# A 7-product block scheme for h = y w_in, with h kept in DRAM, in a fused attention and two-MLP kernel

## The chip, the cores and the metric

The kernel runs on one core of one Trainium2 chip. The metric is the device time of one execution in microseconds (us). PE is TensorE (matmul), DVE VectorE, ACT ScalarE, POOL GpSimd, and SP the engine that issues most DMAs. Each engine, and each DMA queue, works through its own instructions in order.

## What is computed

```
x = attention(q, k, v)      # 4 batches, 8 heads, 576 positions, head size 64, window of 64 -> 2304 tokens x 512
a = x @ w1; b = x @ w2      # 512 x 1024 each
y = ((a * b) @ w3) @ w_out  # 1024 x 1024, 1024 x 512
h = y @ w_in                # 512 x 2048
g = maximum(0.01 * h, h)
out = g @ w_out2            # 2048 x 512 -> 2304 x 512
```

The inputs q, k, v are float32, the weights are 64-bit floats, the output is float32.

## The kernel before

Outside the attention every matrix product is formed from split operands: a float32 value is stored as a rounded high part (fp32r) and the remainder as a low part, and `mm3` issues three matmuls, high x low, high x high, low x high, into one PSUM tile. A split is one copy on ACT (high) and one subtraction on DVE (low). The 64-bit weights are converted on the chip in units of 128 x 512 values: a DMA (`raw`, 512 KB), one ACT scaling (`f`), two bit operations and one shift on DVE, then the split. `advance` moves this pipeline by one unit.

The program has four parts in order:

1. A front of some 150 us: attention of batch 0, w3 w_out folded into one matrix (`wf`), w1 and w2 converted.
2. Four batches of 16 steps. A step is half a batch (288 tokens) and one of eight 128-row tiles f: `ab_step` for a, `ab_step` for b, and with a lag of two steps `y_step`, which adds this tile's share into four PSUM tiles of y. Three `slot()` calls in a step issue the pieces of the next batch's attention; for batches 1 to 3 the transposed probabilities go through DRAM (`pd` out, `pts` in, on SP), and the matmul `pa` that uses them is issued five slots after the store. After the eighth tile ACT copies the four y tiles into `io` tiles (two buffers) and ACT's queue stores them to `yd` in DRAM.
3. In the last batch, which has no attention beside it, w_in and w_out2 are converted (32 units), and the loads and splits of the first y block begin.
4. For six blocks of 384 tokens and 16 tiles f of the 2048 columns: `h_step` (12 matmuls of 384 columns, then ACT scaling, DVE maximum, ACT copy, DVE subtraction, which gives g) and two steps later `o_step` (9 matmuls of 512 columns). Blocks 0 and 1 are interleaved. At the end of a block ACT or DVE copies the output tiles into `io`; the last block's three tiles go into buffers of another pool (`xtile`).

The order of the instructions on an engine follows the order of the calls, moved by priorities (`first`, `high_priority`) and a scheduler.

Of the kernel before, what the change touches and what calls it, by code (L numbers as in the profile page):

```python
# [20 lines left out]
def tile_kernel(ctx: ExitStack, tc: tile.TileContext, q, k, v, w1, w2, w3, w_out, w_in, w_out2, out):  # L21
# [12 lines left out]

    nc = tc.nc
    B, H, S, D = q.shape
    T = B * S
# [17 lines left out]
    W2N = 4  # L55
# [20 lines left out]
    wpool = ctx.enter_context(tc.tile_pool(name="wpool", bufs=1))  # L76
    dram = ctx.enter_context(tc.tile_pool(name="dram", bufs=1, space=bass.MemoryType.DRAM))

    yd = dram.tile([P, KD, T], F32, name="yd")

    stage = tc.alloc_tile_pool(name="stage", bufs=2, side="right")
    att = tc.alloc_tile_pool(name="att", bufs=2, side="right", reuse_waits="tile")
# [3 lines left out]
    xpool = tc.alloc_tile_pool(name="xpool", bufs=8)  # L86
# [21 lines left out]
    def xtile():  # L108
        return xpool.tile([P, 2, S], F32R, name="x", tag="x")
# [8 lines left out]
    def raw_tiles(n):  # L118

        if 0 < n < NHP - 1:  # L120
            t = xpool.tile([P, 2, S], F32, name="x", tag="x")
            return t[:, 0], t[:, 1]
        return tuple(att.tile([P, S], F32, name=x, bufs=1) for x in ("qin", "kin"))
# [8 lines left out]
    def loads_v(n):  # L132
        b, hp = divmod(n, NHP)
        if n < NHP and n >= 2:
            vt = xpool.tile([P, 2, 2, (S - W) // P, D], F32, name="x", tag="x")
        else:
            vt = att.tile([P, 2, 2, (S - W) // P, D], F32, name="vt", bufs=2)
# [62 lines left out]
    def tp(g):  # L200
# [5 lines left out]
        sp.dma_start(pd, tb)  # L206
# [5 lines left out]
    def av(g):  # L212
# [11 lines left out]
        if (b, hp) not in xt:  # L224
            xt[b, hp] = xtile()
# [6 lines left out]
    def wslot(key):  # L232
        pl, tag, bufs = wpool, "w", 8
        if key[0] in ("win", "wo2") and key[1] < W2N // 2:
            pl, tag, bufs = pb1, "w2", W2N
        elif key[0] == "wf" or key[0] in ("win", "wo2") and key[1] >= KF2 // 2 - 2:
# [24 lines left out]
    def feed():  # L261

        while n_of["load"] < min(len(units), n_of["bits"] + RAW):
            load_unit()

    def load_unit():
# [3 lines left out]
        return sp.dma_start(u["raw"], u["src"]).ins  # L270
# [4 lines left out]
    def advance(stop):  # L275

        now = dict(n_of)
        if now["scale"] < min(stop, now["load"]):
# [4 lines left out]
            act.mul(u["f"], u["hi"].bitcast(F32), 2.0 ** -112)  # L283
# [78 lines left out]
    for p in range(KF2 // 2):  # L362
        col_units(w_in, "win", p)
        for h in range(2):
            row_unit(w_out2, "wo2", 2 * p + h)
# [91 lines left out]
    def ab_step(b, hf, f, j):  # L457
# [8 lines left out]
        if j == 0:  # L466
            pss["a"] = gp.tile([P, NH], F32, name="a32", tag="a32", bufs=1)
            with first():
                act.copy(pss["a"], ps)
# [26 lines left out]
    ysp = {}  # L496

    def load_y(c, kk):
        ysp[c, kk] = pb1.tile([P, NB2], F32, name="yr", bufs=1)
        sp.dma_start(ysp[c, kk], yd[:, kk, c * NB2:(c + 1) * NB2])  # L500

    def split_y(c, kk):
        yr, t = ysp[c, kk], xtile()
        act.copy(t[:, 0, 0:NB2], yr)
        dve.tensor_tensor(out=t[:, 1, 0:NB2], in0=yr, in1=f32(t[:, 0, 0:NB2]), op=ALU.subtract)
        ysp[c, kk] = t

    ysteps = []
    for b in range(B):
        if b + 1 < B:  # L510
            plan_att(b + 1, *((10, 26) if b == 0 else (1, 37)))
        for s in range(2 * KF):
# [6 lines left out]
            if b == B - 1:  # L519
                for _ in range(2):  # L520
                    advance(len(units))
                if 4 <= s < 4 + KD:
                    load_y(0, s - 4)
                if 5 <= s < 5 + KD:
                    split_y(0, s - 5)
# [8 lines left out]
        if b == B - 2:  # L534
            att.release()
            ps_at.release()
            ps_h = tc.alloc_tile_pool(name="ps_h", bufs=2, space=PSUM, side="right", reuse_waits="tile")
            pb1 = tc.alloc_tile_pool(name="pb1", bufs=W2N, side="right", reuse_waits="tile")
# [3 lines left out]
    gp.release()  # L542
    ps_mm.release()
    ps_ab.release()
    pb2 = tc.alloc_tile_pool(name="pb2", bufs=2, reuse_waits="tile")
    ps2 = tc.alloc_tile_pool(name="ps2", bufs=6, space=PSUM, reuse_waits="tile")


    g_t = {}

    def h_step(c, f):
        ps = ps_h.tile([P, NB2], F32, name="h")
        w = cols2(slots["win", f // 2])
        ws = slice(P * (f % 2), P * (f % 2) + P)
        with tc.issue_after(pss["last"]) if c == 0 and f < 2 else nullcontext():
            for kk in range(KD):
                y = ysp[c, kk]
                mm3(ps, w[:, 0, kk, ws], w[:, 1, kk, ws], y[:, 0, 0:NB2], y[:, 1, 0:NB2], kk == 0, kk == KD - 1)
# [82 lines left out]
```

## Time and profile before

| quantity | value |
|---|---|
| median of 3 runs | 888.66 us (888.52 to 888.69) |
| profiled execution | 888.87 us |
| its span (first to last instruction) | 887.1 us |
| PE busy | 847.2 us, 96% |
| DVE busy | 466.9 us, 53% |
| ACT busy | 338.7 us, 38% |
| POOL busy | 43.5 us, 5% |
| mean granted TensorE clock | 0.987 of full speed |

The span leaves out 1.8 us of the profiled execution. Matmuls overlap, so that their durations add up to more than the time they take together: the spacing from start to start (the pitch) is what one costs in a full stream. The same holds, more weakly, for DVE.

### The profile page before, as it was taken

Reading aid. Unit: us, or ns where it says so; the run is one execution under the profiler, and the core shown is the slowest. Engines: PE = TensorE matmul, PEld = TensorE weight load, DVE = VectorE, ACT = ScalarE, POOL = GpSimd, SP = SyncE. Lnnn points to the kernel's source line nnn. Section 1 sums busy time; section 2 is a strip of 40 time slices with the busy share of each in tenths; the row PEclk is TensorE's granted clock in tenths of the full one; section 3 lists DMA queues with packets and bytes.
Section 4 is the critical chain, followed back from the end, with each engine's and each line's share of the span. In section 5 each row is a group of like instructions: output and inputs, shape, how many; then the busy total and the mean of one; then the engine's idle time right before and its main releaser. Section 6 shows DMA issues by size and latency. Waiting matters only on the chain.

```text
span 887.1 us, 14660 instructions
## 1 busy us (share of the span) xinstructions
PE 847.2 (96%) x5476; PEld 778.1 (88%) x5476; DVE 466.9 (53%) x1231; ACT 338.7 (38%) x890; POOL 43.5 (5%) x61
## 2 busy tenths in 40 slices
PE   5779787999999999999999999999999999999997
PEld 3568686999999999999999899999899999999996
DVE  7999898763665365539298922233223223223222
ACT  4466653442434243436165622233223223222221
POOL 1012000110111011100000000000000000000000
PEclk9899998899999999999999999999999999999999
DMA  7897668666555444415256300012001001000000
GB/s 239 214 208 225 168 183 196 173 163 134 125 113 137 98 105 103 113 46 182 71 168 203 100 0 1 1 30 88 27 1 44 28 1 36 28 1 13 24 0 36
DMA packets 166822, 84.84 MB, mean 96 GB/s; under 512 B 133216, under 2 KB 153184, under 8 KB 166752
## 3 DMA queue, kind: packets, MB, share of 16 engines
q1 hardware_dynamic: 162144, 79.20, 33.8%
q10 hardware_dynamic: 4608, 4.72, 1.6%
q8 instruction: 43, 0.70, 0.3%
q14 instruction: 27, 0.22, 0.1%
HBM read 67.37 MB, written 16.52 MB: 95 GB/s over the span
## 4 chain that ended last, share of the span: by engine, by line
PE 81%; DMA 8%; DVE 5%; SPq 2%; ACT 2%; issue 1%; DVEq 0%; ACTq 0%
PE o L72 7%; PE o L73 7%; PE o L71 7%; PE h L73 7%; PE h L71 7%; PE h L72 7%; PE ab L71 7%; PE ab L73 6%; PE ab L72 6%; PE mm L71 4%; PE mm L73 4%; PE mm L72 4%; PE sc L168 3%; DMA raw<-in_moe_w_dram 3%; PE pa L222 2%; DMA raw<-in_moe_w_out_dram 2%
## 5 line engine op out<-in xcount | busy, mean ns | idle before, releaser
L71 PE MATMUL ab<-x,w 128*128 128x288 f32 x512 | 154.7, 303 | 5.1 <-ACT x L228 3.0
L563 DVE TENSOR_TENSOR t<-h,t 128x384 f32<-128x384 f32 x95 | 52.9, 557 | 197.2 <-ACT t L562 197.2
L72 PE MATMUL ab<-x,w 128*128 128x288 f32 x512 | 152.3, 297 | 0.0
L73 PE MATMUL ab<-x,w 128*128 128x288 f32 x512 | 152.2, 297 | 0.0
L562 ACT ACTIVATE t<-h 128x384 f32<-128x384 f32 x95 | 46.7, 491 | 192.9 <-PE h L73 191.3
L71 PEld LDWEIGHTS ab<-x,w 128*128 128x128 f32 x512 | 97.4, 190 | 7.0 <-ACT x L228 3.1
L72 PEld LDWEIGHTS ab<-x,w 128*128 128x128 f32 x512 | 97.3, 190 | 0.2
L73 PEld LDWEIGHTS ab<-x,w 128*128 128x128 f32 x512 | 97.3, 190 | 0.1
L73 PE MATMUL h<-x,w 128*128 128x384 f32 x288 | 97.0, 337 | 0.0
L71 PE MATMUL h<-x,w 128*128 128x384 f32 x288 | 96.9, 336 | 0.0
L72 PE MATMUL h<-x,w 128*128 128x384 f32 x288 | 96.8, 336 | 0.0
L71 PE MATMUL o<-w,g 128*128 128x512 f32 x213 | 83.3, 391 | 1.0 <-ACT g L564 1.0
L72 PE MATMUL o<-w,g 128*128 128x512 f32 x213 | 84.2, 395 | 0.0
L73 PE MATMUL o<-w,g 128*128 128x512 f32 x213 | 82.6, 395 | 0.0
L565 DVE TENSOR_TENSOR g<-t,g 128x384 fp32r<-128x384 f32 x95 | 53.0, 558 | 45.8 <-ACT g L564 45.8
L71 PE MATMUL mm<-ab,wf 128*128 128x288 f32 x256 | 70.7, 310 | 3.9 <-ACT ab L475 3.9
L283 ACT ACTIVATE f<-raw 128x512 f32<-128x512 f32 x72 | 48.5, 677 | 67.7 <-DMA raw<-in_moe_w_dram 33.1
L73 PE MATMUL mm<-ab,wf 128*128 128x288 f32 x256 | 74.2, 296 | 0.0
L72 PE MATMUL mm<-ab,wf 128*128 128x288 f32 x256 | 74.2, 295 | 0.0
L564 ACT CAST g<-t 128x384 fp32r<-128x384 f32 x95 | 48.7, 513 | 51.6 <-DVE t L563 51.5
L176 ACT ACTIVATE s<-s,nm 128x128 f32<-128x128 f32 x144 | 56.5, 395 | 19.9 <-DVE nm L172 18.7
L474 DVE TENSOR_TENSOR p<-ab,a 128x288 f32<-128x288 f32 x64 | 29.1, 454 | 55.7 <-PE ab L73 53.4
(93 smaller groups left out, 1586.3 us busy)
## 6 DMA issues: line engine op xcount, KB each, us to landing
raw<-in_moe_w_dram SPq DMA_DIRECT2D x32, 512.0 KB, 4.6
raw<-in_moe_w_out_dram SPq DMA_DIRECT2D x24, 512.0 KB, 4.8
raw<-in_moe_w_in_dram SPq DMA_DIRECT2D x16, 512.0 KB, 3.9
vt<-in_v_dram SPq DMA_DIRECT2D x56, 128.0 KB, 2.9
pd<-tb SPq DMA_DIRECT2D x36, 192.0 KB, 2.2
pts<-pd SPq DMA_DIRECT2D x144, 48.0 KB, 2.0
yd<-io ACTq DMA_DIRECT2D x32, 144.0 KB, 2.5
yr<-yd SPq DMA_DIRECT2D x24, 192.0 KB, 2.4
```

The lines of the kernel that those rows point to most:

```text
L71: pe.matmul(ps, lhsT=lh, rhs=rh, start=first, stop=False)
L72: pe.matmul(ps, lhsT=lh, rhs=rl, start=False, stop=False)
L73: return pe.matmul(ps, lhsT=ll, rhs=rh, start=False, stop=last).ins
L168: pe.matmul(sc[:, t, :], lhsT=qb[:, t, :], rhs=kT[n][:, k0:k0 + P], start=True, stop=True)
L176: act.activation(out=s[:, t, :], in_=s[:, t, :], func=AF.Exp, bias=nm[:, t:t + 1], scale=-1.0, accum_out=sm[:, t:t + 1])
L222: pe.matmul(o[W * h:W * h + W, W * t:W * t + W], lhsT=vt[:, a, h, m, :], rhs=pts[:, 2 * h:2 * h + 2, t], start=True, stop=True)
L283: act.mul(u["f"], u["hi"].bitcast(F32), 2.0 ** -112)
L474: dve.tensor_tensor(out=p32, in0=ps, in1=pss["a"], op=ALU.mult)
L562: act.mul(t, ps, 0.01)
L563: dve.tensor_tensor(out=t, in0=ps, in1=t, op=ALU.max)
L564: act.copy(g[:, 0], t)
L565: dve.tensor_tensor(out=g[:, 1], in0=t, in1=f32(g[:, 0]), op=ALU.subtract)
```

## The change

The matrices of h = y w_in are cut into blocks. A quad is a pair of adjacent 128-column tiles of w_in (8 pairs `p`) by a pair of 384-token blocks (3 pairs `c`), and the contraction of 512 is cut into two halves. Of such a 2 x 2 by 2 x 2 block product the standard form has 8 block products; the change uses the 7-product form with 4 sums of w_in blocks, 4 sums of y blocks and 7 sums after the products. A product is 6 matmuls of 384 columns.

- `keep`: 28 units (all 16 of w_in, 12 of the 16 of w_out2) are converted but not split. They are stored as float32 in DRAM (`wd`), from step 4 of the third batch on. The other 4 are converted while output is formed.
- `w_ops(p)`: loads two units, forms 4 sums in `io` tiles, splits 7 blocks. `y_ops(c, j)`: loads four y blocks, forms 4 sums, splits 7 blocks, with the low parts on POOL for the last token pair. For the first token pair and the first w_in pair they stand in the steps of the last batch.
- `Quad.step`: one product, and the additions into float32 tiles `c`, out of PSUM, on DVE (the first one a copy on ACT); finished blocks of h are stored to `hd` by SP.
- After all 24 quads come the 96 output steps: `ahead` loads h four steps ahead, splits g two steps ahead, and loads and splits the kept w_out2 rows in the steps of block 0. `o_step` is as before, but the last block's tiles go through `io` as well.
- Buffers: the x tiles are in two pools of four (`xa`, `xb`), and other pools are released earlier.

```diff
+    def keep(i):
+        return lambda f: sp.dma_start(wd[i], f)
...
-            if b == B - 1:
-                for _ in range(2):
-                    advance(len(units))
...
+            if 2 * KF * b + s >= 2 * KF * (B - 2) + 4:
+                for _ in range(2 if b == B - 1 and s < 4 else 1):
+                    advance(KEPT)
+            if b == B - 1 and n_of["fin"] == KEPT and len(early) > 0:
+                early.pop(0)()
...
+    def y_ops(c, j):
...
+        for o, x0, x1 in ((t1, b12, b11), (t2, b22, t1), (t3, b22, b12), (t4, b21, t2)):
+            dve.tensor_tensor(out=o, in0=x0, in1=x1, op=ALU.subtract)
+        for i, x in enumerate((b11, b21, b22, t1, t2, t3, t4)):
+            act.copy(t[:, i, j, 0], x)
+            (pool if c == NP - 1 else dve).tensor_tensor(out=t[:, i, j, 1], in0=x, in1=f32(t[:, i, j, 0]), op=ALU.subtract)
...
+    def w_ops(p):
...
+        for h in range(2):
+            sp.dma_start(u[h].rearrange("p k c m -> p (k c m)"), wd[2 * p + h])
+        a11, a21, a12, a22 = u[0][:, :, 0], u[0][:, :, 1], u[1][:, :, 0], u[1][:, :, 1]
+        sums = [stage.tile([P, 2, 2, P], F32, name="io", tag="io", bufs=2) for _ in range(2)]
...
+        for j, x in enumerate((u[1].rearrange("p k c m -> p c k m"), sums[0], sums[1], a11.unsqueeze(1))):
+            t = w_tile(p, j)
...
+            act.copy(h, x)
+            dve.tensor_tensor(out=l, in0=x, in1=f32(h), op=ALU.subtract)
...
+        def product(self, m):
+            n_of["bank"] += 1
+            pool = ps_h if n_of["bank"] % 8 in (1, 2) else ps2
...
+            for j in range(2):
+                ws = slice(P * j, P * j + P)
+                pss["last"] = mm3(ps, w[:, 0, ws], w[:, 1, ws], y[:, b, j, 0], y[:, b, j, 1], j == 0, j == 1)
...
+            if of is None:
+                act.copy(self.sb[to], ps)
+            else:
+                dve.tensor_tensor(out=self.sb[to], in0=ps, in1=self.sb[of], op=ALU.add)
...
-    def h_step(c, f):
...
+    def ahead(i):
+        if i < len(steps):
+            c, f = steps[i]
+            load_h(c, f)
+            if c == 0 and f < KEEP2:
+                load_w(f)
+        if SPLITS <= i < len(steps) + SPLITS:
+            c, f = steps[i - SPLITS]
+            with first():
+                if c == 0 and f < KEEP2:
+                    split_w(f)
+                split_h(c, f)
...
+    w_ops(1)
+    for i in range(0, len(quads), 2):
...
+        for k in range(7):
+            for q in quads[i:i + 2]:
+                with first():
+                    q.step(k)
+            if i // 2 < NP - 1 and k in (0, 1):
+                y_ops(i // 2 + 1, k)
...
+    for i, (c, f) in enumerate(steps):
+        ahead(i + LOADS)
+        if i == 0:
+            n_of["cap"] = len(units)
+            feed()
+        if i >= 8 and c < 2:
+            advance(len(units))
+        if c == 0 and f >= KEEP2:
+            until(last["wo2", f], len(units))
+        o_step(c, f)
```

Three places of the program order follow. The first is ACT at the end of the last batch. Before, the copies of the last four y tiles (`io`, from `mm`) and their stores (`yd`) stand among conversions (`f`, `w`, `wf`) and the first h steps (`h`, `t`, `x`):

```order
L493 COPY io_6150<-mm_5794 128x288
L493 COPY io_6153<-mm_5798 128x288
L494 DMA yd_63<-io_6150 128x288
L494 DMA yd_63<-io_6153 128x288
L564 CAST x_6200<-x_6199 128x384
L562 ACTIVATE t_6223<-h_6210 128x384
L283 ACTIVATE f_5947<-raw_5891 128x512
L493 COPY io_6156<-mm_5802 128x288
L493 COPY io_6159<-mm_5806 128x288
```

Now, on the same engine, the first two copies and stores (`io_6147`, `io_6150`) stand a few rows ahead of these; behind the last two come the high parts (`w1_6183`, `w2_6186`) of two sums of the second w_in pair, which lie in the next two `io` tiles (`io_6174`, `io_6175`); `pr` are products, `yop1` the operands of the second token pair:

```order
L561 CAST w0_6180<-f_6171 128x2x256
L561 CAST w3_6189<-f_6170 128x256
L535 CAST yop1_6192<-f_6211 128x384
L535 CAST yop1_6192<-raw_6219 128x384
L513 COPY io_6153<-mm_5798 128x288
L513 COPY io_6156<-mm_5802 128x288
L514 DMA yd_63<-io_6153 128x288
L514 DMA yd_63<-io_6156 128x288
L639 COPY c_6209<-pr_6202 128x384
L535 CAST yop1_6192<-f_6215 128x384
L561 CAST w1_6183<-io_6174 128x2x256
L561 CAST w2_6186<-io_6175 128x2x256
```

The sums of the w_in pair take the place of the conversions, and use the tiles that the y stores use. On PE, four products stand between the last y matmul (`mm_5802`) and the first matmul that reads `w1_6183` (product `pr_6248`).

The second place is DVE where the output begins. Before, it starts with conversions and splits of weights (`f`, `wf`), the splits of y (`x`), and the maxima and low parts (`t`, `g`) of the first h steps side by side:

```order
L563 TENSOR_TENSOR t_6223<-h_6210,t_6223 128x384
L296 TENSOR_SCALAR f_5947<-f_5947 128x512
L253 TENSOR_TENSOR wf_5949<-f_5874,wf_5949 128x512
L563 TENSOR_TENSOR t_6249<-h_6236,t_6249 128x384
L299 SCALAR_TENSOR_TENSOR f_5938<-raw_5881,f_5938 128x512
L253 TENSOR_TENSOR wf_5949<-f_5883,wf_5949 128x512
```

Now the products end there. Rows with `w2` are low parts of w_out2 rows, rows with `f` conversions, `t` and `g` the h steps; the row `g_8121` is the low part that the third output step waits for:

```order
L260 TENSOR_TENSOR w2_8262<-f_8217,w2_8262 128x512
L260 TENSOR_TENSOR w2_8262<-f_8260,w2_8262 128x512
L260 TENSOR_TENSOR w2_8295<-f_8227,w2_8295 128x512
L260 TENSOR_TENSOR w2_8295<-f_8246,w2_8295 128x512
L305 TENSOR_SCALAR f_8271<-f_8271 128x512
L305 TENSOR_SCALAR f_8293<-f_8293 128x512
L302 SCALAR_TENSOR_TENSOR f_8271<-raw_8061,f_8271 128x512
L684 TENSOR_TENSOR g_8082<-t_8081,g_8082 128x384
```

The conversions and splits of w_out2, which were spread over the last batch and the interleaved steps of blocks 0 and 1, now stand ahead of the low parts of g.

The third place is SP in the third batch. Before, the stores (`pd`) and reloads (`pts`) of the probabilities follow one another:

```order
L206 DMA pd_4686<-tb_4684 128x384
L209 DMA pts_4688<-pd_4686 32x4x96 x4
L206 DMA pd_4797<-tb_4795 128x384
L209 DMA pts_4799<-pd_4797 32x4x96 x4
L206 DMA pd_4866<-tb_4864 128x384
```

Now the stores of converted units (`wd`) and loads of new ones (`raw`) stand between them:

```order
L278 DMA raw_4398<-in_moe2_w_in_dram 128x2x256
L374 DMA wd_65<-f_4313 128x512
L213 DMA pd_4417<-tb_4415 128x384
L278 DMA raw_4488<-in_moe2_w_in_dram 128x2x256
L374 DMA wd_65<-f_4392 128x512
L216 DMA pts_4419<-pd_4417 32x4x96 x4
L374 DMA wd_65<-f_4482 128x512
L213 DMA pd_4538<-tb_4536 128x384
```

Of the 28 stores ten stand ahead of the last `pts` reload.

## Rows read from the trace of the kernel before

**Rows 1.** The page, part 1: busy us (share of the span) x instructions.

```profile
PE 847.2 (96%) x5476; PEld 778.1 (88%) x5476; DVE 466.9 (53%) x1231; ACT 338.7 (38%) x890; POOL 43.5 (5%) x61
```

**Rows 2.** Busy time by window; then granted clock, DMA share, GB/s.

```profile
309.00:395.00 86.00, 86.00 (x738) 83.46 (x737) 44.74 (x169) 32.61 (x121) 9.92 (x12) 1.00 0.38 95
500.00:882.30 382.30, 382.27 (x1915) 345.27 (x1913) 118.55 (x215) 105.77 (x214) 0.00 (x0) 1.00 0.06 19
```

**Rows 3.** Groups by form: busy us, mean ns; idle before. One of three h lines.

```profile
L73 PE MATMUL h<-x,w 128*128 128x384 f32 x288 | 97.0, 337 | 0.0
L73 PE MATMUL h<-x,wf 128*128 128x384 f32 x96 | 32.4, 337 | 0.0
```

**Rows 4.** Timeline of PE: start, duration; firsts of 12 h, 9 o, next h.

```profile
601.81 0.33 PE L71 MATMUL h<-x,wf 128*128 128x384 f32 x1
...
603.92 0.39 PE L71 MATMUL o<-wf,g 128*128 128x512 f32 x1
...
606.00 0.33 PE L71 MATMUL h<-x,wf 128*128 128x384 f32 x1
```

**Rows 5.** Timeline of PE where the output begins; [idle before <-releaser].

```profile
485.12 0.50 PE L71 MATMUL o<-w,x 128*128 128x512 f32 x1 [0.70 <-ACT x L564]
490.79 0.50 PE L71 MATMUL o<-w,g 128*128 128x512 f32 x1 [1.04 <-ACT g L564]
```

**Rows 6.** Timeline of PE: its three longest waits after the first 10 us.

```profile
31.69 1.08 PE L330 MATMUL ab<-ident,f 128*128 128x128 f32 x4 [2.89 <-DVE f L299]
106.35 0.99 PE L71 MATMUL ab<-x,w 128*128 128x288 f32 x2 [3.00 <-ACT x L228]
150.48 1.11 PE L71 MATMUL mm<-ab,wf 128*128 128x288 f32 x4 [3.54 <-ACT ab L475]
```

**Rows 7.** Windows just behind these three waits, columns as in Rows 2.

```profile
32.00:38.50 6.50, 5.95 (x17) 4.46 (x16) 6.31 (x14) 3.55 (x6) 0.00 (x0) 0.53 0.97 263
106.30:109.70 3.40, 3.35 (x16) 2.97 (x17) 2.25 (x5) 0.99 (x2) 0.00 (x0) 0.51 0.93 229
150.40:160.90 10.50, 10.42 (x44) 9.00 (x45) 7.19 (x23) 2.69 (x10) 1.09 (x1) 0.52 0.65 137
```

**Rows 8.** Timeline of DVE, three instructions back to back.

```profile
474.91 0.69 DVE L253 TENSOR_TENSOR w<-f,w 128x512 fp32r<-128x512 f32 x1
475.51 0.55 DVE L505 TENSOR_TENSOR x<-yr,x 128x384 fp32r<-128x384 f32 x1
475.98 0.45 DVE L474 TENSOR_TENSOR p<-ab,a 128x288 f32<-128x288 f32 x1
```

**Rows 9.** DMA issues: count, KB each, median us from issue to landing.

```profile
pd<-tb SPq DMA_DIRECT2D x36, 192.0 KB, 2.2
pts<-pd SPq DMA_DIRECT2D x144, 48.0 KB, 2.0
yd<-io ACTq DMA_DIRECT2D x32, 144.0 KB, 2.5
out_dram<-x SPq DMA_DIRECT2D x3, 256.0 KB, 2.3
```

**Rows 10.** Groups of ACT by form, columns as in Rows 3.

```profile
L493 ACT COPY io<-mm 128x288 f32<-128x288 f32 x32 | 12.1, 393 | 8.3 <-DMA yd<-io 5.0 <-PE ab L73 1.7 <-PE mm L73 1.5
L252 ACT CAST w<-f 128x512 fp32r<-128x512 f32 x48 | 29.1, 619 | 6.6 <-PE ab L73 3.5 <-DVE f L299 3.0
```

**Rows 11.** Timeline of POOL and of DVE at one moment, columns as in Rows 5.

```profile
195.21 0.83 POOL L185 TENSOR_TENSOR s<-s,rs 128x384 f32<-128x384 f32 x1 [3.83 <-DVE rs L184]
...
195.26 1.10 DVE L476 TENSOR_TENSOR ab<-p,ab 128x288 fp32r<-128x288 f32 x1 [0.22 <-ACT ab L475]
```

**Rows 12.** Timeline of the end: last matmuls, copies on DVE, output stores.

```profile
881.43 0.84 PE L73 MATMUL o<-wf,g 128*128 128x512 f32 x3
...
882.26 1.09 DVE L585 COPY x<-o 128x256 f32<-128x256 f32 x3 [3.83 <-ACT x L584]
882.71 1.31 SPq L587 DMA_DIRECT2D out_dram<-x  x3
```

More of the change, by code (lines that the diff above doesn't have):

```diff
@@ L282, in advance @@
             u["f"] = stage.tile([P, UC], F32, name="f", tag="f", bufs=4)
-            act.mul(u["f"], u["hi"].bitcast(F32), 2.0 ** -112)
+            with tc.issue_after(pss["copy"]) if now["scale"] >= PHASE_B else nullcontext():
+                act.mul(u["f"], u["hi"].bitcast(F32), 2.0 ** -112)
             n_of["scale"] += 1
@@ L542, in tile_kernel @@
     gp.release()
+    xb.release()
+    wpool.release()
     ps_mm.release()
     ps_ab.release()
-    pb2 = tc.alloc_tile_pool(name="pb2", bufs=2, reuse_waits="tile")
+    ph = tc.alloc_tile_pool(name="ph", bufs=2, reuse_waits="tile")
     ps2 = tc.alloc_tile_pool(name="ps2", bufs=6, space=PSUM, reuse_waits="tile")
-    g_t = {}
-    def h_step(c, f):
[L552 to L558, printed above, removed]
-        t = f32(xtile()[:, 0, 0:NB2]) if (c, f) == (0, 0) else pb2.tile([P, NB2], F32, name="t")
-        g = xtile()[:, :, 0:NB2] if (c, f) == (0, 0) else pb2.tile([P, 2, NB2], F32R, name="g", bufs=3)
-        with first():
-            act.mul(t, ps, 0.01)
-            dve.tensor_tensor(out=t, in0=ps, in1=t, op=ALU.max)
-            act.copy(g[:, 0], t)
-            dve.tensor_tensor(out=g[:, 1], in0=t, in1=f32(g[:, 0]), op=ALU.subtract)
@@ new lines, in tile_kernel, with load_w, split_w, load_h @@
+    wraw = {}
+    hr = {}
+    g_t = {}
+    def load_w(f):
+        wraw[f] = stage.tile([P, UC], F32, name="f", tag="f", bufs=4)
+        sp.dma_start(wraw[f], wd[KF2 + f])
+    def split_w(f):
+        key = ("wo2", f // 2)
+        if key not in slots:
+            slots[key] = wslot(key)
+        store(key, f % 2)(wraw[f])
+    def load_h(c, f):
+        hr[c, f] = po1.tile([P, NB2], F32, name="h", bufs=4)
+        sp.dma_start(hr[c, f], hd[:, f, c * NB2:(c + 1) * NB2])
+    def split_h(c, f):
+        h = hr.pop((c, f))
+        t = po1.tile([P, NB2], F32, name="t", bufs=2)
+        g = po1.tile([P, 2, NB2], F32R, name="g", bufs=3)
+        act.mul(t, h, 0.01)
+        dve.tensor_tensor(out=t, in0=h, in1=t, op=ALU.max)
+        act.copy(g[:, 0], t)
+        dve.tensor_tensor(out=g[:, 1], in0=t, in1=f32(g[:, 0]), op=ALU.subtract)
@@ L597, in tile_kernel @@
-    for i in range(len(steps) + LAG):
-        for c, kk in loads.get(i, []):
-            load_y(c, kk)
-            split_y(c, kk)
+    def ahead(i):
         if i < len(steps):
             c, f = steps[i]
-            if i < len(both):
-                until(max(last[n, f // 2] for n in ("win", "wo2")), len(units))
-                advance(len(units))
-            h_step(c, f)
-        if i >= LAG:
-            o_step(*steps[i - LAG])
-    for p in (ps_h, ps2, pb2, pb1, xpool, stage):
+            load_h(c, f)
[7 more added lines that the diff above has]
+                split_h(c, f)
@@ new lines, in tile_kernel @@
+    order = [(p, c) for c in range(NP) for p in range(2)] + [(p, c) for p in range(2, NF) for c in range(NP)]
+    quads = [Quad(p, c) for p, c in order]
+    w_ops(1)
+    for i in range(0, len(quads), 2):
+        if i // 2 < NP - 1:
+            yop[i // 2 + 1] = ph.tile([P, 7, 2, 2, NB2], F32R, name=f"yop{i // 2 + 1}", bufs=1)
+        for k in range(7):
[4 more added lines that the diff above has]
+                y_ops(i // 2 + 1, k)
+            if k == 3:
+                for p in {q.p + 1 for q in quads[i + 2:i + 4]} | {q.p for q in quads[i + 2:i + 4]}:
+                    if p not in wop and p < NF:
+                        w_ops(p)
+        if i == len(quads) - 4:
+            yb0.release()
+            po1 = tc.alloc_tile_pool(name="po1", bufs=4, side="right", reuse_waits="tile")
+            for n in range(LOADS):
+                ahead(n)
```

140 lines of the change are left out of this document (100 added, 40 removed).

## The prediction

> **What bounds the kernel now.** I read the page's shares first: PE is busy for 96% of the span, DVE for 53% [rows 1]. A share over stages says little, so I read windows next: in the third batch PE is busy for 86.00 of 86.00 us, and in the long middle of the h and output steps for 382.27 of 382.30 us, at a granted clock of 1.00 [rows 2]. DVE is busy for 44.74 us of the first and 118.55 us of the second window. So behind the front, PE bounds, and what counts is how many matmuls there are and what one costs. Durations do not tell that, because matmuls overlap: a 384-column one lasts 0.337 us [rows 3], but twelve of them run from 601.81 to 603.92, a pitch of 0.1758 us, and nine 512-column ones from 603.92 to 606.00, 0.2311 us [rows 4]. In the same way I read DVE from start to start: in a row a 128x512 instruction costs 0.60 us (duration 0.69) and a 128x384 one 0.47 us (duration 0.55) [rows 8].
>
> Waits of PE are rare behind the front: two where the output begins, 0.70 and 1.04 us, for g [rows 5]. The three longest in the front are 2.89, 3.00 and 3.54 us [rows 6], and behind each the granted clock is 0.51 to 0.53 for 6.5, 3.4 and 10.5 us [rows 7], the lower of the two levels, 1.2 instead of 2.4 GHz. The waits of 0.70 and 1.04 us lost no clock. So a wait of some 3 us is paid twice.
>
> **What the change removes.** h has 3 lines x (288 + 96) = 1152 matmuls of 384 columns [rows 3]. The 24 quads have 24 x 7 x 6 = 1008 (the order of the changed program has 1008 as well). The 144 that go are worth 144 x 0.1758 = 25.3 us. The 864 output matmuls stay. The two waits at the first output steps go with their place: -1.7 us. Below I ask at each seam what is late instead.
>
> **Third and fourth batch: +1.0 (0 to 5).** Conversion now starts in the third batch. Some 12 units, each with two 128x512 instructions and a shift on DVE (2 x 0.60 + at most 0.60 us), add up to 22 us to 44.74 of 86 us: DVE has room, and PE hides it. In the fourth the splits of weights go and sums come; DVE does not rise by more than it has idle. What can be late is a queue: SP waits for a converted unit before its `wd` store, and behind that stand `pd` and `pts`. A slot is 86 / 48 = 1.79 us. Five slots, 9.0 us, less the transposition (at most 0.69), 2.2 for `pd` and 2.0 for `pts` [rows 9], leave 4.1 us of slack for each attention group. The low end is that all is covered. For the high end I let a few of the groups be late by a microsecond. I take 1.0, near the low end, since DVE stays at (44.74 + 22) / 86 = 78% of the window.
>
> **Seam from y to the products: a wait of 2.9 us.** This is the one stall that the order makes nearly certain. There are two `io` buffers. The last four y tiles go through them, and then the sums of the second w_in pair. From the end of the last matmul of the first y tile the chain is: copy 0.39 [rows 10], store to landing 2.5 [rows 9], copy of the third tile 0.39, store 2.5, two sums at some 0.35 (a 256-column instruction, estimated from the 0.47 of 384 columns), high part 0.62 [rows 10]: 7.1 us. For eight handovers I add 0.1 us each, as at the end, where the first output store is issued 0.09 us after the first of three DVE copies (882.26 + 0.36 to 882.71) [rows 12]: 7.9 us. Meanwhile PE has six more y matmuls (some 0.13 each) and 24 product matmuls x 0.1758: 5.0 us. So PE waits 2.9 us for `w1_6183`; without handovers 2.1, and 4.5 if a store lands late.
>
> Such a wait is as long as the shortest of the three in rows 6, and all three cost clock. Half speed for 6.5, 3.4 or 10.5 us loses half of that: 3.2, 1.7 or 5.2 us. I take the middle one, +3.2.
>
> **First token pairs: +2.0 (0 to 9).** After that DVE has a heavy stretch: from the last sum of the second w_in pair to the second sum of the third token pair there are 52 instructions, 41 of 384 columns, 5 of 512, 6 of 256: at the pitch 41 x 0.47 + 5 x 0.60 + 6 x 0.35 = 24.4 us, at durations 28.5 us. A high part on ACT (some 0.5) and a low part on POOL (0.83, as POOL's multiplication of the same size [rows 11]) follow: 25.7 or 29.8 us. PE's products up to the first one that reads it are 147 x 0.1758 = 25.8 us, and PE starts some 0.4 us later: it waits 0 at the pitch and 3.6 us at durations. Then POOL's chain costs 0.83 for each operand and PE uses one for two quads in 6 x 0.1758 = 1.05 us, so it keeps ahead. But DVE and POOL disturb each other: at 195.26 a subtraction beside POOL's instruction took 1.10 us [rows 11] instead of 0.45 [rows 8]. Twelve instructions with both inputs in SBUF lie beside POOL's fourteen; were each delayed like a milder one by 0.45, that is 5.4 us, which makes the high end 9. Most of the 64 subtractions of that line are not disturbed, and eight product banks let DVE lag in its sums; I take 2.0, nearer to the low end.
>
> The Trainium skill says on this, in "SBUF — State Buffer", section "Who interferes with whom", that a DVE instruction with two SBUF inputs and a GpSimd instruction that reads SBUF share a port, and whichever starts first blocks the other for its whole length. By that rule POOL is held up as well, the fourteen low parts moved to POOL relieve DVE less than the count shows, and the sum would be some 4 us higher. The one row fits the rule; how often they meet in the changed program no row shows.
>
> **The products between the seams: 0.** A pair of quads is 14 x 6 x 0.1758 = 14.8 us of PE. DVE has 14 additions x 0.47 = 6.6 us and one set of weight operands, some 4 us. PE hides both. Were DVE to stop for a moment, eight product tiles give 8 us of cover.
>
> **Seam from the products to the output: +2.8 (0 to 7.4).** From the last addition that waits for the product `pr_7859` to the low part `g_8121`, DVE has 54 instructions: 27 of 384 columns, 23 of 512, 4 short ones: 27 x 0.47 + 23 x 0.60 + 4 x 0.35 = 27.9 us, at durations 32.5 us. PE has 86 x 0.1758 + 43 x 0.2311 = 25.1 us until it needs that low part. So PE waits 2.8 us at the pitch, 7.4 us at durations, nothing if the scheduler's lead is larger than I see. DVE's instructions are back to back there, so I take the pitch. I count no second fall of the clock, since the wait comes in two or three pieces. Behind it, DVE's two instructions of g stand against nine output matmuls of 2.08 us: hidden.
>
> **End: +1.2 (0.5 to 2).** The last three output tiles come out of PE by 882.27; their stores are issued from 882.71 on, and the span ends at 887.1 [rows 12]. Now there are two buffers: the third copy waits until the first store has landed, 882.7 + 2.3 [rows 9] = 885.0, then 0.4 for the copy, 0.1, and 2.3 for its own store: 887.8 to 888.8, if the first takes a microsecond more.
>
> **Sum.** Against the profiled execution of 888.87 us: - 25.3 - 1.7 + 1.0 + 2.9 + 3.2 + 2.0 + 2.8 + 1.2 = 875.0. That execution is 0.2 us over the median of the runs (888.66), so the forecast is 874.8 us.
>
> **Rivals.**
>
> *Smooth seams, clock kept.* The chain over `io` takes its low end, 2.1 us, which lies nearer to the 1.04-us wait that lost no clock than to 3.54, and the two DVE stretches keep up: 888.9 - 25.3 - 1.7 + 2.1 + 0.5 and 0 to 3 for the rest = 865 to 868; I put it at 866. For it: PE can be three steps ahead of DVE anywhere between. Against it: the chain is made of two landings in a row, and a landing is not shortened by anything.
>
> *DVE becomes the bound at both seams.* Its instructions take their durations instead of the pitch, and POOL delays some: 1.6 + 4.6 us more are 881, with all of POOL's delay 886; I put it at 883. For it: both stretches wait on other engines, so that instructions do not always follow back to back. Against it: rows 8 are such a mixed stretch, and the pitch held there.
>
> *Slower than before: SP's queue holds the attention back.* In the third batch nine `pd` stores have a `wd` store ahead of them. If SP stands for longer than the 4.1 us of slack, `pa` is late, PE, in order, stops, and the price is paid nine times. From 874.8 to 888.7 there are 13.9 us, 1.5 us per group: it decides from a hold of 5.6 us on. At 6 us it is 9 x 1.9 = 17 us, 892 us. For it: ACT's scaling and DVE's bit operations of a unit stand in order behind other waits. Against it: DVE has a fifth of its time free there, and raw loads are issued four units ahead.
>
> *It does not do what it says.* The count of matmuls is in the order, so the 25.3 us go in any case; only waits can give them back, and those are the rivals above.
>
> **How the numbers follow.** Forecast, with or without the fall of the clock in its usual size (870 to 880): 0.48. Smooth seams, 866: 0.27. DVE-bound, 883: 0.17. SP's queue, 892: 0.06; other mishaps 0.02. The range of 8 in 10 takes the forecast whole, nearly all of the smooth case and most of the DVE case: 865 to 885. A difference under 0.2% (1.8 us) is no change that a measurement of this kernel can tell. Faster by more: the first two cases and nearly all of the third, 0.90; no change 0.03, the edge of the third and a milder fourth; slower 0.07.
>
> **What would show it.** 1008 product matmuls at a pitch of 0.176 us in the middle of the product phase, PE without waits there. One wait of about 3 us before the first matmul with `w1`, ended by the ACT copy of a sum, with the `io` store as what DVE waited for; behind it a window at half the clock. Waits of some 2 us for POOL or DVE at the third token pair, and for `g` at the third output step. `pa` without waits in the third and fourth batch. The last output store issued near 885.5 on the scale of before, two microseconds after the others. The prediction is wrong if PE waits repeatedly inside the products, if the third batch is longer than 86 us by more than 5, or if the wait at the first seam costs no clock.

## The result, and the profile after

The changed kernel takes 874.18 us (median; 873.42 to 875.67) against 888.59 us, a ratio of 0.9844 (0.9827 to 0.9862). Timed a second time it took 873.24 against 885.08 us, 0.9863 (0.9827 to 0.9899); the kernel before spread from 878.8 to 889.9 us there, the changed one from 871.5 to 873.6. The forecast was 874.8 us. The sum is right; several of its terms are not, and what they missed cancels, so that the closeness of the number is luck in good part.

The profiled execution took 874.35 us, its span is 872.6 us. The page's shares, to be laid beside [rows 1]:

```profile
PE 824.2 (94%) x5332; PEld 750.1 (86%) x5332; DVE 583.9 (67%) x1475; ACT 369.5 (42%) x948; POOL 61.4 (7%) x75
```

144 matmuls fewer, 117 us more of DVE. Then the windows of the changed kernel (columns as in [rows 2]): the stretch that answers to the last line of [rows 7], the third batch, the first seam, the third token pair, the middle of the products, the second seam in two parts, the output.

```profile
150.40:160.90 10.50, 10.50 (x87) 9.46 (x86) 8.15 (x30) 4.41 (x18) 1.65 (x2) 1.00 0.69 175
309.00:395.00 86.00, 86.00 (x743) 83.22 (x742) 61.89 (x201) 40.23 (x131) 9.73 (x11) 1.00 0.74 204
473.10:488.00 14.90, 11.25 (x62) 10.59 (x62) 10.25 (x22) 8.36 (x18) 0.00 (x0) 1.00 0.40 120
513.00:523.00 10.00, 8.23 (x42) 6.87 (x41) 9.03 (x15) 2.53 (x6) 5.14 (x5) 1.00 0.73 245
545.00:650.00 105.00, 104.29 (x596) 103.88 (x595) 61.80 (x130) 17.19 (x34) 0.00 (x0) 1.00 0.39 133
650.00:662.20 12.20, 10.13 (x48) 9.14 (x47) 9.18 (x19) 7.02 (x14) 0.00 (x0) 0.86 0.73 236
662.20:684.00 21.80, 19.27 (x78) 13.84 (x78) 20.39 (x40) 12.02 (x24) 0.00 (x0) 1.00 0.44 146
684.00:865.00 181.00, 181.00 (x786) 147.49 (x785) 97.89 (x176) 92.97 (x180) 0.00 (x0) 1.00 0.38 112
```

The reader is to see three things. From 150.4 to 160.9 us the clock is whole, where it was 0.52: that the forecast did not have. PE is full in the third batch, in the middle of the products and in the output. What it loses it loses at the places named, and more there than forecast. The waits of PE at the two seams, by the timeline:

```profile
474.99 0.44 PE L75 MATMUL pr<-yop,w 128*128 128x384 f32 x1 [1.88 <-ACT w L561]
480.46 0.44 PE L75 MATMUL pr<-yop,w 128*128 128x384 f32 x1 [0.97 <-ACT w L561]
487.83 0.44 PE L75 MATMUL pr<-yop,w 128*128 128x384 f32 x1 [0.80 <-DVE c L641]
657.36 0.44 PE L75 MATMUL pr<-yop,w 128*128 128x384 f32 x1 [2.06 <-DVE c L641]
670.48 0.50 PE L75 MATMUL o<-w,g 128*128 128x512 f32 x1 [1.49 <-ACT g L683]
679.00 0.50 PE L75 MATMUL o<-w,g 128*128 128x512 f32 x1 [0.71 <-ACT g L683]
```

And the end, which answers to [rows 12]: the last matmuls, and the third copy, on ACT and on DVE, behind a store:

```profile
865.31 0.86 PE L77 MATMUL o<-w,g 128*128 128x512 f32 x3
...
868.74 0.37 ACT L702 COPY io<-o 128x256 f32<-128x256 f32 x1 [2.36 <-DMA out_dram<-io]
869.15 0.42 DVE L703 COPY io<-o 128x256 f32<-128x256 f32 x1 [2.25 <-ACT io L702]
```

To compare runs stage by stage I take four marks from each trace: the start of the last y matmul, of the last product matmul, of the last output matmul, and the span's end (us). By the pitch of [rows 4] the products need 1002 x 0.1758 = 176.1 us behind the last y matmul (in e6 1140 x 0.1758 = 200.4, in e8 996 x 0.1758 = 175.1, since twelve product matmuls stand ahead of that mark there), the output 199.6. From the last output matmul to the end the kernel before needs 5.2 us.

| kernel | median | last y | products | output | end |
|---|---|---|---|---|---|
| changed | 874.2 | 472.8 | 189.4 | 203.6 | 6.8 |
| e3, own tiles | 870.2 | 469.8 | 186.6 | 203.3 | 5.2 |
| e4, conversion pinned | 868.5 | 470.7 | 189.6 | 199.5 | 6.8 |
| e5, low parts on DVE | 881.2 | 472.7 | 192.8 | 206.6 | 6.8 |
| e6, eight products | 887.9 | 473.8 | 204.6 | 200.9 | 6.8 |
| e7, e3 + e4 | 866.3 | 472.7 | 185.9 | 200.2 | 5.2 |
| e8, first quad first | 870.0 | 475.2 | 184.3 | 204.1 | 5.2 |
| e9, e7 and two edits | 864.9 | 471.1 | 186.8 | 200.1 | 5.2 |

The last y matmul of the changed kernel started at 470.9 us in its second trace, so that two microseconds in that column are not the work of an edit. What the marks lose against the pitch (us) shows the place better. The product matmuls are counted: up to the 60th, the 252nd, the 948th and the last; then the output.

| kernel | first seam | token pairs | middle | second seam | output |
|---|---|---|---|---|---|
| changed | 3.3 | 4.8 | 1.1 | 4.0 | 4.0 |
| changed, second trace | 3.6 | 5.2 | 1.1 | 4.7 | 3.4 |
| e3 | 4.7 | 1.0 | 0.6 | 4.2 | 3.7 |
| e4 | 3.3 | 5.9 | 1.1 | 3.2 | -0.1 |
| e5 | 3.2 | 7.3 | 1.7 | 4.5 | 7.0 |
| e7 | 4.7 | 0.7 | 0.6 | 3.8 | 0.6 |

### The profile page after: what moved, and what is told of

Its sections match the earlier page's. It is cut to its first block, busy times and chain, and to the rows that moved or that the text cites. A ratio compares the mean times of both kernels' runs of the same rounds, so it can differ in the third digit from the quotient of the medians.

```text
span 872.6 us, 15307 instructions
## 1 busy us (share of the span) xinstructions
PE 824.2 (94%) x5332; PEld 750.1 (86%) x5332; DVE 583.9 (67%) x1475; ACT 369.5 (42%) x948; POOL 61.4 (7%) x75
## 5 line engine op out<-in xcount | busy, mean ns | idle before, releaser
L641 DVE TENSOR_TENSOR c<-pr,c 128x384 f32<-128x384 f32 x168 | 83.4, 549 | 50.9 <-PE pr L77 38.2
L75 PE MATMUL o<-w,g 128*128 128x512 f32 x288 | 113.6, 394 | 2.2 <-ACT g L683 2.2
L76 PE MATMUL o<-w,g 128*128 128x512 f32 x288 | 113.2, 393 | 0.0
L75 PE MATMUL pr<-yop,w 128*128 128x384 f32 x324 | 102.3, 343 | 8.6 <-DVE c L641 4.8
L76 PE MATMUL pr<-yop,w 128*128 128x384 f32 x324 | 101.3, 339 | 0.2 <-POOL yop L536 0.2
L77 PE MATMUL pr<-yop,w 128*128 128x384 f32 x324 | 97.2, 339 | 0.0
L77 PE MATMUL o<-w,g 128*128 128x512 f32 x288 | 83.1, 394 | 0.3 <-DVE g L684 0.2
L76 PE MATMUL mm<-ab,wf 128*128 128x288 f32 x256 | 74.4, 294 | 0.9 <-DVE ab L496 0.9
L681 ACT ACTIVATE t<-h 128x384 f32<-128x384 f32 x96 | 50.3, 525 | 56.8 <-DVE g L684 53.7
L77 PE MATMUL mm<-ab,wf 128*128 128x288 f32 x256 | 74.3, 294 | 0.0
L75 PE MATMUL mm<-ab,wf 128*128 128x288 f32 x256 | 73.4, 309 | 0.0
L75 PEld LDWEIGHTS pr<-yop,w 128*128 128x128 f32 x324 | 60.3, 189 | 12.6 <-DVE c L641 7.3
L75 PEld LDWEIGHTS o<-w,g 128*128 128x128 f32 x288 | 54.2, 188 | 15.9 <-ACT g L683 3.5
```

The source lines that it names most:

```text
L75: pe.matmul(ps, lhsT=lh, rhs=rh, start=first, stop=False)
L76: pe.matmul(ps, lhsT=lh, rhs=rl, start=False, stop=False)
L77: return pe.matmul(ps, lhsT=ll, rhs=rh, start=False, stop=last).ins
L641: dve.tensor_tensor(out=self.sb[to], in0=ps, in1=self.sb[of], op=ALU.add)
L681: act.mul(t, h, 0.01)
```

## The experiments

**The front.** Between the 144th and the 192nd matmul of a and b the kernel before needs 142.4 to 163.4 us, the changed one 142.4 to 155.8. ACT of the kernel before, in that stretch (timeline):

```profile
148.30 0.66 ACT L283 ACTIVATE f<-raw 128x512 f32<-128x512 f32 x1 [3.05 <-DMA raw<-in_moe_w_out_dram]
148.86 0.39 ACT L176 ACTIVATE s<-s,nm 128x128 f32<-128x128 f32 x1
...
150.01 0.42 ACT L475 CAST ab<-p 128x288 fp32r<-128x288 f32 x1
```

A scaling of a unit that is wanted 250 us later has been moved ahead into batch 0, and ACT, in order, waits 3.05 us for its load; the exponentials and the copy for which PE waits 3.54 us [rows 6] stand behind it. The change orders such scalings behind the latest copy of a. e1 gives the kernel before that line alone, e2 takes it from the changed kernel:

```diff
# e1, the kernel before (and pss["copy"] = act.copy(pss["a"], ps).ins in ab_step)
-            act.mul(u["f"], u["hi"].bitcast(F32), 2.0 ** -112)
+            with tc.issue_after(pss["copy"]) if now["scale"] >= PHASE_B else nullcontext():
+                act.mul(u["f"], u["hi"].bitcast(F32), 2.0 ** -112)
# e2, the changed kernel: the reverse
```

> The kernel before with one line of the change alone: ACT's scaling of a w_in or w_out2 unit is ordered behind the latest copy of a. The comparison of the two traces shows the 7.6 us that the change gains between 142 and 163 us (the wait of 3.54 us at 150.48 and the window at half clock behind it). Theory A: without that line the scheduler puts scalings of w_in and w_out2 units into batch 0, ACT, in order, waits there for their loads (3.05 us at 145 to 148), and behind it stand the exponentials and the copy that PE waits for. Then the wait falls below 1.5 us, the clock between 150 and 161 us stays at 1.00, and the time is 880.5 to 884 us. Rival B: the gain came from the other order of loads on SP (k loads ahead of a weight load) or from the split x pools, which this kernel doesn't have: the time stays within 1.5 us of 888.6 and the wait stays above 2.5 us.

e1: 882.78 us (881.4 to 883.6) against 887.13, ratio 0.9951 (0.9935 to 0.9968). The windows of e1:

```profile
144.00:150.00 6.00, 6.00 (x44) 5.40 (x43) 2.56 (x7) 1.59 (x8) 0.00 (x0) 1.00 0.87 200
150.00:160.00 10.00, 9.20 (x79) 8.59 (x79) 7.27 (x29) 4.20 (x18) 1.65 (x2) 1.00 0.73 164
```

The wait and the half clock are gone, the 192nd matmul starts at 157.4 us. Theory A holds. Against the 888.6 us of the first measurement it is the size expected; against the kernel before as timed beside e1 (887.13) the median moved by 4.4 us.

> The changed kernel without that same line (scalings may be moved ahead again), all else as changed. Theory A: scalings move into batch 0, a wait of 2 us or more comes back near 147 to 150 us, and the time rises by 4 to 8 us to 878 to 882. Rival B (order of loads or the x pools made the gain): the time stays within 1.5 us of 874.2. If it moves less than A says but scalings do stand early, the k loads that the change issues earlier are a second part of the gain.

e2: 884.49 us (880.0 to 888.8), 10 us above the changed kernel. PE waits 2.67 us at 148.52 behind a scaling again, and 2.68 us in the third batch (388.01), where a scaling holds ACT up for 2.90 us:

```profile
148.52 1.19 PE L75 MATMUL mm<-ab,wf 128*128 128x288 f32 x4 [2.67 <-ACT ab L495]
```

Behind a wait of 1.74 us in the fourth batch (439.12) stand copies of y operands that wait 1.70 us for their load, and no scaling. The line is worth more than theory A said: by the 768th matmul of a and b e2 is 1.6 us behind the changed kernel, by the 1488th 11.3, so that most of it lies in the two batches of conversion. Of the 7.6 us between the 144th and the 192nd matmul e1 gains 6.9 and e2 gives back 4.3, in one trace each; for the rest the k loads that the change issues earlier stay a rival.

**The first seam and the end.** e3:

```diff
-        sums = [stage.tile([P, 2, 2, P], F32, name="io", tag="io", bufs=2) for _ in range(2)]
+        tag, n = ("raw", RAW) if p == 1 else ("io", 2)
+        sums = [stage.tile([P, 2, 2, P], F32, name=tag, tag=tag, bufs=n) for _ in range(2)]
...
-                o = stage.tile([P, DM], F32, name="io", tag="io", bufs=2)
+                tag, n = ("io", 2) if c < NC2 - 1 else ("f", 4)
+                o = stage.tile([P, DM], F32, name=tag, tag=tag, bufs=n)
```

> The changed kernel, in which the four sums of the second w_in pair lie in tiles of the weight loads instead of the two that the y stores use, and the last three output tiles lie in tiles of their own. Theory: both chains of stores go: the wait of 0.97 us for the second w_in pair (480.46) vanishes, the last output copy no longer waits 2.36 us for a store, and the time falls by 2.5 to 4 us to 870 to 872, 1.5 us of it at the end. Rival: the stretch up to the third token pair is bound by DVE and POOL, so what is gained at 475 to 481 us is lost again by 520 us; then only the end's 1.5 us remain, 872.7 us.

e3: 870.22 us (866.7 to 872.2); 2.8 us fewer in the products, 1.6 fewer at the end (tables). The chain over `io` is gone, but not the wait:

```profile
473.02 0.44 PE L75 MATMUL pr<-yop,w 128*128 128x384 f32 x1 [2.92 <-ACT w L562]
```

PE now waits once, for the high part of another operand of the same w_in pair. ACT's timeline has ahead of it two copies of y (0.70), two store issues on ACT's queue (0.81) and a copy of a product. So the seam had two chains, and the forecast had seen one. The gain has the size expected but not the place: the seam itself loses more than before (4.7 us against 3.3), with the clock at 0.51 from 474.5 to 477, and what is gained lies in the token pairs behind it (1.0 against 4.8). In the changed kernel DVE stands for 2.23 us ahead of the sums (478.87); the copy on ACT that the profile names had ended at 477.90, which leaves the landing of the stores issued at 476.10. In e3 this wait is gone, and PE is full beside POOL's low parts and behind them:

```profile
488.00:513.00 25.00, 25.00 (x145) 25.00 (x144) 23.24 (x45) 9.51 (x20) 16.52 (x14) 1.00 0.69 228
513.00:523.00 10.00, 9.93 (x57) 9.62 (x56) 6.38 (x13) 1.67 (x4) 0.00 (x0) 1.00 0.93 323
```

So the chain over `io` was paid at the third token pair, by way of DVE.

**The second seam.** e4 adds one word of order: the last conversions come behind the latest g.

```diff
-        act.copy(g[:, 0], t)
+        pss["copy"] = act.copy(g[:, 0], t).ins
```

> The changed kernel, in which the conversion of the last four w_out2 units is ordered behind the high part of the latest g, so that it can't be moved ahead of the first output steps. Theory: these twelve DVE instructions, 6 us, stand among the last additions and the first low parts, and make DVE late at the seam to the output. Without them the waits of 2.06, 1.49 and 0.71 us (657 to 679) shrink to 2 us together, the clock stays at 1.00 from 658 to 661, and the time falls by 3 to 5 us to 869 to 871. Rival: the additions and the twelve w_out2 low parts alone keep DVE behind; the waits keep two thirds of their length and the time falls by 1 us or less.

e4: 868.46 us (868.1 to 869.1), half a microsecond below the expectation. Of the 6.0 us between the two profiled executions 2.1 lie ahead of the last y matmul, where the edit changes nothing. Two windows of e4, up to the first output matmul and behind it:

```profile
650.00:660.20 10.20, 7.72 (x41) 6.76 (x41) 8.33 (x17) 5.57 (x12) 0.00 (x0) 1.00 0.70 237
660.20:682.00 21.80, 21.64 (x97) 17.69 (x96) 15.92 (x31) 11.11 (x22) 0.00 (x0) 1.00 0.50 155
```

PE is idle for 0.2 us there instead of 2.5, DVE is busy for 15.9 us instead of 20.4, and the output takes 4.1 us less (table). More moved than the twelve conversion instructions: seven of the sixteen low parts of w_out2 stand behind 680 us as well, so the gain is that of all nineteen, and the twelve alone are not tested. The wait of 2.06 us inside the last products stays (656.21); the clock is 1.00 behind it, where the changed kernel shows 0.50 from 658 to 661, and that this is the edit's doing is not shown (last section). What DVE does ahead of that wait the changed kernel's timeline shows:

```profile
651.11 0.56 DVE L682 TENSOR_TENSOR t<-h,t 128x384 f32<-128x384 f32 x1 [1.50 <-ACT t L681]
...
654.61 0.69 DVE L260 TENSOR_TENSOR w<-f,w 128x512 fp32r<-128x512 f32 x1 [1.80 <-ACT w L259]
```

Both belong to the first output steps and stand ahead of the last additions; ACT in turn waits for the load of h (2.46 us) and of a w_out2 row (1.73 us).

**POOL and DVE.** e5:

```diff
-            (pool if c == NP - 1 else dve).tensor_tensor(out=t[:, i, j, 1], in0=x, in1=f32(t[:, i, j, 0]), op=ALU.subtract)
+            dve.tensor_tensor(out=t[:, i, j, 1], in0=x, in1=f32(t[:, i, j, 0]), op=ALU.subtract)
```

> The changed kernel with the fourteen low parts of the third token pair on DVE instead of POOL. In the trace of the changed kernel POOL's and DVE's instructions lengthen one another there (POOL 1.16 to 1.18 us each instead of 0.83, DVE's two-input sums up to 1.3 instead of 0.55), and between 513 and 523 us PE loses 3 us. Theory (they block each other, so POOL is no relief): DVE gets 14 x 0.47 = 6.6 us more but loses no time to POOL, some 6 us; the time stays within 1 us of 874.2. Rival A (POOL is a net loss): 871.5 to 873. Rival B (POOL is a true relief and DVE is short there): 6 us more DVE work is late, 877 to 880.

e5: 881.22 us (877.9 to 882.9), above the range of rival B: POOL is a true relief, although the two do block each other. Groups of the changed kernel, 495 to 520 us, and then the line of additions out of PSUM over the whole kernel (min/median/max ns):

```profile
L536 POOL TENSOR_TENSOR yop<-raw,yop 128x384 fp32r<-128x384 f32 x8 | 9.3, 1181 | 2.2 <-ACT yop L535 2.1
L536 POOL TENSOR_TENSOR yop<-f,yop 128x384 fp32r<-128x384 f32 x6 | 8.2, 1379 | 119.9 <-DVE c L641 117.4 <-ACT yop L535 2.5
L533 DVE TENSOR_TENSOR raw<-f,raw 128x384 f32<-128x384 f32 x4 | 3.7, 932 | 0.0
L533 DVE TENSOR_TENSOR raw<-f 128x384 f32<-128x384 f32 x4 | 3.2, 802 | 0.7 <-DMA f<-yd 0.7
...
L641 DVE TENSOR_TENSOR c<-pr,c x168: 544/548/559, 481.4 to 667.6; 128x384 f32<-128x384 f32 x168
```

POOL needs 1.18 to 1.38 us; beside additions alone such a low part took 1.01 (e3, 491.93), so that this, and not the 0.83 of another operation [rows 11], is its undisturbed time. DVE's sums with both inputs in SBUF take 0.80 to 0.93 instead of 0.55. The additions, with one input in PSUM, are not disturbed: the fourteen of the 168 that lie beside a POOL instruction took 0.545 to 0.553 us. That is the rule of the Trainium skill, "SBUF — State Buffer", section "Who interferes with whom" (a DVE instruction with two SBUF inputs and a GpSimd instruction that reads SBUF contend for a shared port), and the trace agrees. But what DVE loses by it, some 2.5 us over these sums and 1.5 over two instructions of 256 columns (1.14 and 1.22 us instead of 0.42), is less than the 14 x 0.47 = 6.6 us that it is spared. e5 loses 2.5 us more at the token pairs and 3.0 more in the output, where PE waits 5.70 us at the first output matmul (671.53) for an addition on DVE. The second part is no debt carried along: DVE is busy for only 66.7 of the 115 us from 525 to 640, and its last addition ends 5.9 us behind the start of the last product matmul in both kernels. Why PE waits for it in e5 alone these runs do not show.

**What the seven products bring.** e6 keeps all but the form: two products accumulate in one tile, four copies go out. Of its edit the core:

```diff
+            for kh in range(2):
+                w, y = wop[self.p][fh if kh else 2 + fh], yop[self.c]
+                for j in range(2):
...
+            (dve.tensor_copy if k % 2 else act.copy)(self.sb[n], ps)
```

> The changed kernel with eight products for each quad, two accumulated in one product tile: no sums of operands, no additions afterwards, four copies out. 1152 instead of 1008 matmuls; all else (h by way of DRAM, conversion ahead, seams) as changed. Theory: the seven-product form saves 25.3 us of PE, but its sums and additions cost some 8 us of waits (3 at the third token pair, 2 in the middle, 3 where the output begins), so this kernel takes 874.2 + 25.3 - 8 = 891 us (888 to 894). Rival A: the waits come from stores, loads and conversions, not from the sums, and stay: 898 to 901. Rival B: DVE was the bound of the whole product phase and most of the 25 us is given back: 884 us or less.

e6: 887.87 us (886.2 to 891.2), just below the range of the theory, between it and rival B. Its windows in the products and in the output:

```profile
490.00:677.00 187.00, 186.66 (x1064) 185.78 (x1063) 37.50 (x70) 36.19 (x76) 7.09 (x8) 1.00 0.39 132
...
690.00:878.00 188.00, 188.00 (x817) 153.28 (x816) 103.72 (x187) 97.45 (x189) 0.00 (x0) 1.00 0.37 111
```

DVE is busy for 20% there, and PE waits nowhere for more than 0.3 us behind 477 us until the output. The product stage takes 204.6 us, 4.1 more than its work. In the changed kernel it takes 189.4, 13.2 more than its work: of the 25.3 us of PE, 9.1 are given back in waits that come with the sums and additions (the chain over `io` among them, which e6 has not either), and 2.6 in the output. That leaves 13.6 us, and the medians differ by 13.7: so much the form is worth as built. Beside e6 the kernel before took 886.01 us, a ratio of 1.0022 (1.0006 to 1.0039): without the form the rest of the change costs 1.9 us, although the front gains by it.

**Together.** e7 is e3 and e4 in one; e8 and e9 go on from e7.

```diff
# e8: the first quad's seven products ahead of the second's
-            for q in quads[i:i + 2]:
+            for q, m in [(quads[0], k)] if i == 0 else [(q, k) for q in quads[i:i + 2]]:
...
+                with first(), tc.issue_after(end0):
+                    quads[1].step(m)
# e9: last half batch, and no priority for the first four splits
+                    end = b == B - 1 and hf == 1
+                    (dve.tensor_copy if end else act.copy)(y, yps[j][:, 0:NH])
+                    (sp if end else act).dma_start(yd[:, j, t0:t0 + NH], y)
...
+            with first() if i >= LOADS else nullcontext():
```

> Both edits together: the tiles of e3 (own tiles for the sums of the second w_in pair and for the last three output tiles) and the pin of e4 (the last four conversions behind the latest g). Theory: they act in different places (475 to 481 us and the end; 653 to 680 us), so that their gains in those stretches add: 2.8 + 2.1 + 3.6 us, 874.2 - 8.5 = 865.7 us (864 to 868). Rival: the gain at the first seam only brings PE earlier to the additions that wait for DVE, so that half of it is lost again at the output: 868 to 870.

e7: 866.33 us (863.8 to 869.2), ratio 0.9782 (0.9752 to 0.9812). The gains add: 3.5 us in the products, 3.4 in the output, 1.6 at the end; the edits alone gave 2.8 in the products and 1.6 at the end (e3) and 4.1 in the output (e4).

> e7, and in the first pair of quads all seven products of the first quad stand ahead of those of the second. In e3 PE waits 2.92 us (473.02) for the high parts of the second w_in pair, which on ACT stand behind the copies of y and can't begin before the last y matmul, since their tiles reuse memory of the batches. Theory: six products of the first quad, 6 us, whose operands are ready, cover that: the wait shrinks below 0.7 us and the time falls by 2 to 3 us below e7, 863 us. Rival: with all additions of one quad in a row, DVE and the eight product tiles become short, or the wait reappears at the second quad, and the time stays within 1 us of e7.

e8: 870.02 us (869.4 to 872.2). The rival, and worse. At the first seam PE still waits 1.85 us (479.57). The products are 1.6 us shorter, 1.1 of it only because six more product matmuls stand ahead of the last y matmul; two waits (1.39 and 2.03 us, 658.6 and 661.9) are followed by 0.50 of the clock until 667 us, and the output takes 204.1 us. The last y matmul comes 2.6 us later than in e7, 1.1 of it for those six; the rest is no more than the front varies by.

> The changed kernel once more, unaltered, so that it and the kernel before are timed together in as many rounds as the experiments were: the kernel before spread over 882 to 889.7 us there. Both theories on where the gain comes from expect 872 to 877 us. If the changed kernel spreads as the kernel before does, the front (before 160 us) varies in both; if it stays within 2 us, the pinned scaling takes the variation out as well.

The changed kernel stayed within 2.1 us, the kernel before spread over 11. e1, with the pin alone, stayed within 2.2, and e2, without it, spread over 8.7: the pinned scaling takes out most of the variation. Not all of it: e3, e5, e6 and e7 have the pin and spread over 5.0 to 5.5 us.

> e7 with two more edits, in two places. In the last half batch DVE instead of ACT copies the four y tiles, and SP instead of ACT stores them: ACT is then free for the high parts of the second w_in pair, for which PE waits 2.92 us in e7 (475.88), behind two copies, two store issues (0.81 us) and a copy of a product. Theory: the wait shrinks to 1.5 us or less and the clock behind it stays at 1.00, 2.5 to 3.5 us in all. And the first four splits of w_out2 and g are no longer given priority over the last additions, ahead of which they wait for loads on ACT and DVE (2.23 us at 650.95 in e7, and half clock behind it). Theory: that wait shrinks below 1 us, 2 us in all, but the first output steps may wait 1 us longer for g. Together 861 to 863 us. Rival: DVE takes over what ACT loses, and the splits are late for the output: the waits move behind 480 and 659 us and the time stays within 1.5 us of e7 (866.3).

e9: 864.91 us (863.3 to 866.0), 1.4 below e7, a difference that its trace has in the front (last y at 471.1). The rival: both waits moved on.

```profile
483.67 0.69 PE L75 MATMUL pr<-yop,w 128*128 128x384 f32 x1 [3.15 <-ACT c L641]
...
655.50 0.44 PE L75 MATMUL pr<-yop,w 128*128 128x384 f32 x1 [3.00 <-DVE c L643]
```

## Why the prediction was right, and where it was not

- **25.3 us of matmuls**: right. The products run at the pitch, 1002 of them.
- **Third and fourth batch, +1.0**: right. From the 768th to the 1488th matmul of a and b 160.2 us against 159.8; SP's queue held nothing back, and that rival is out.
- **Not in the sum: the front, -6.1.** 7.6 us gained at 147 to 160 and 1.5 lost near 202. The row stood in [rows 6, 7] and I used it as a price only; I did not ask whether the change alters what stands ahead of it on ACT. e1 and e2 show that it does, by one line of order that I had read as a side matter.
- **First seam, 2.9 us**: 1.88 + 0.97 = 2.85 us, the right size, but in two waits by two chains. The second is the one over `io`; the first I had not seen.
- **3.2 us of clock**: not at this seam in the first trace, where the clock stayed whole. In the second trace of the same program it fell behind the same wait of 1.88 us, and yet the seam lost 3.6 us instead of 3.3, for the wait of 0.97 us behind it is gone there:

```profile
473.07 0.44 PE L75 MATMUL pr<-yop,w 128*128 128x384 f32 x1 [1.88 <-ACT w L561]
...
474.00:476.00 2.00, 2.00 (x8) 2.00 (x7) 0.71 (x2) 0.44 (x2) 0.00 (x0) 0.50 0.41 104
```

So the fall of the clock came there, and cost 0.3 us since the second chain covered the rest. In e3, where one wait of 2.92 us is left with half the clock behind it, the seam loses 4.7 us, so that the fall cost at most 1.8 and not 3.2. At the second seam the clock fell for some 3 us in both traces.
- **First token pairs, +2.0**: too small, 4.8 by the start times. I had put the mutual blocking of POOL and DVE near nothing, and POOL's fourteen low parts took 17.5 us instead of 14 x 0.83 = 11.6. But they took as long in e3, where PE loses 1.0 us: blocking alone does not make the loss, it needs the late start that the chain over `io` gives DVE. That the chain would be paid there I had not seen.
- **Second seam, +2.8**: too small by more than half. By the start times 4.0 us go inside the last products (the wait of 2.06 us and the clock) and 4.0 in the output (1.49 and 0.71 us and smaller ones). I had asked only when the third output step gets its low part. e4 shows that the second part came of weight instructions on DVE, conversions and low parts, which I had counted, but at the pitch.
- **End, +1.2**: 1.6 (6.8 against 5.2 us).

Behind the last y matmul 13.2 + 4.0 = 17.2 us are lost, forecast 10.9 with the clock. That is the rival "DVE becomes the bound at both seams" in good part, and without the front's 6.1 us the time would have been 880 us, near the lower end that it was given (881). So the forecast hit since a gain that it had not seen made up for losses that it had put too low. By its own signs it was wrong in two points: PE waits repeatedly inside the products (487.83, 520.08, 657.36), and the wait at the first seam cost no clock in the first trace. What e4 does not explain of the second seam, the 2.06 us inside the last products, moved in e9 and did not go: in e9 DVE still stands for 2.24 us (651.68) for the high part of a w_out2 row, which waits for its load. That these instructions of the output steps make the wait is read from the timeline; no run took it away.

## What to carry to other kernels

When a change trades matmuls for sums, price the sums at the places where the operands of a stage are first made and where the last results leave it; in the middle they are hidden. A wait need not be paid where it is made: the chain over `io` was, for the most part, paid some 40 us later. Look in the order for instructions that have nothing to wait for but a load: a scheduler moves them far ahead, and an in-order engine then waits for the load in front of urgent work; one ordering edge (4.4 us in e1, 4.1 in the output of e4) was worth about a third of the 13.7 us that the new form is worth. And two chains at one seam can hide each other: taking one away (e3, e9) shows the next.

## What the hardware showed unexpectedly

The clock behind a wait. PE's wait of 1.88 us at the first seam was followed by a granted clock of 1.00 in one trace of the changed kernel (474.99) and of 0.50 in the other (473.07): the same program, the same wait. Waits of 1.85 us in e8 (479.57), 2.06 in the changed kernel (657.36), 2.08 in e6 (476.15), 2.23 in e7 (650.95) and 2.57 in e3 (648.76) were followed by 0.50 as well. But 2.06 us in e4 (656.21), 2.31 in the kernel before (58.98), and 3.00 in e9 (655.50) were not: 1.00 all through. So between 1.85 and 3.00 us neither the length of a wait nor the program decides, and my reading of [rows 6, 7], that a wait of some 3 us is paid twice, was too firm. What else decides, these runs do not tell apart.
